# A linear-attention block and its MLP: rows of four steps, the two lowest levels inside a row

## The chip, the cores and the metric

The kernel runs on one core of a Trainium2 chip. The metric is device time in microseconds of one execution; lower is better. All times of the kernel before come from three runs and from one profiled execution.

## What is computed

Inputs r, k, v, w have the shape (batch 4, heads 8, steps 768, head size 48), u is (8, 48). The result of the attention, its heads side by side, is x of shape (4, 768, 384), and a normalized MLP of width 1536 is added to it.

```python
for t in range(S):
    cur = einsum('bhd,bhe->bhde', u[None] * k_t, v_t)
    y[:, :, t] = einsum('bhd,bhde->bhe', r_t, state + cur)
    state = w_t[..., None] * state + einsum('bhd,bhe->bhde', k_t, v_t)
...
x = y.transpose(0, 2, 1, 3).reshape(B, S, H * D)
mu, var = x.mean(-1), ((x - mu) ** 2).mean(-1)
xn = (x - mu) / sqrt(var + 1e-06) * g_ln
out = x + maximum(xn @ w_ch1, 0) @ w_ch2
```

So a value of step s reaches the output of a later step t through the product of k_s, of r_t and of every w between them, and reaches its own step through u.

## The kernel before

**Blocks and rounds.** The steps of a batch are cut in two halves of 384 steps (`RN`, three tiles of 128). A half with all eight heads is a round; there are eight rounds, and a round has two units of four heads, each with two pairs of heads. Round 0 is worked in two parts, its first tile and the other two. Where the prediction speaks of blocks, it means rounds.

**Inside a tile.** A tile of 128 steps is two chunks of 64 (`C`). Within a chunk the matrix of weights between steps is built in six levels (`NLEV`). At level `lev` steps stand in groups of n = 2^lev, and the matrix gets the squares between each even group and the odd group after it. `quads` makes the products of k and r for all squares of a level in small-tile form on TensorE (48 products for a whole round), into one of two PSUM places named `a`. `keep` copies the wanted squares from PSUM into the matrix `A` in SBUF: level 0 by an AND with a mask, levels 1 to 4 with a predicated copy, and level 5 by `keep_last` on ScalarE. `grow` then multiplies half of k and half of r by the products of w over the neighbouring group, so that the next level can be made from them. These products of w, for groups of 1, 2, 4 up to 32 steps, are made by `totals` on VectorE or GpSimd; those over 64 steps are `decay`.

**Loading and turning.** `load` brings w, k and r in their natural order, steps on partitions, into the `nat` places; in rounds 0 and 1 each partition gets three neighbouring steps of a head, later one step of each tile. `turn` transposes all three on TensorE into `w`, `k`, `r` with two heads and their 48 numbers on partitions; ScalarE copies the result from PSUM. In rounds 0 and 1 a transpose takes two instructions.

**The own step.** `own` makes the products r k u of each step and adds them over the 48 numbers (three VectorE or GpSimd instructions for half a round). In rounds 0 and 1 `own_by_tile` writes the sums to DRAM and reads them back by tile. `own_term` multiplies them with v, and the outputs' last step adds this to what TensorE made (`x<-a,vo` in the profile).

**State and outputs.** `turn_k` turns k back, `states` makes the sums of k and v per chunk and `decay` carries them on; `outputs` takes the matrix `A` with v, and r with the states, into an `a` place. Then come normalization, three transposes a tile, and the MLP. From round 1 on the MLP's first matrix is used in three parts, one of which, `d`, is streamed from DRAM for each of its twelve pieces (`stream`), into the eight `rest` places. From round 5 on the second matrix is in three parts too. At the start the two matrices, 64-bit numbers in DRAM, are made into 32-bit numbers on ScalarE and VectorE (`convert`).

**Order.** Nothing is issued where it is written. Each step is an `Op` of the class `Plan`, with an engine or a choice of engines, a cost, what it reads and writes, the places it takes and a priority, 40 for each round plus a stage. `Plan.order` simulates the engines and picks the op with the lowest priority number among those that can start first. The order found this way is fixed for each engine, the DMA issues on SyncE (`SP`) among them. The table `SHIFTS` moves priorities, by their whole number. Products with two operands in SBUF on VectorE and GpSimd are kept apart in time (`port`). In the first 90 us, where TensorE would wait, it runs filler products named `idle`. All instructions go through `InOrder`, so the profile shows line 50 for nearly all of them, and groups are told apart by tile names.

Of the kernel before, what the change touches and what calls it, by code (L numbers as in the profile page):

```python
# [66 lines left out]
class Plan:  # L67
# [23 lines left out]
        -472: 60.5, -360: -211.5, -38: -20.5, -32: -113.5, -31: -113.5, -29: -113.5, -22: -111.5,  # L91
        -20: -12, -10: 118.5, -6: 46.5, 8: -1.5, 9: 93.5, 11: -340.5, 12: -313.5, 16: 6.5, 20: 17,
        22: -346.5, 38: 25.5, 43: 250.5, 44: -325, 47: 80.5, 48: -87, 50: 79.5, 52: 93, 54: 95,
        56: 134, 58: 6, 60: 40, 62: 32, 66: -60.5, 83: 279, 87: 298.5, 88: 39, 90: 33, 92: 89,
        98: -296.5, 100: 100.5, 128: 801.5, 134: -18.5, 141: 36, 142: 138.5, 168: -69, 169: -48.5,
        170: 4.5, 178: 16, 180: -201.5, 182: 54, 184: 37, 200: 340.5, 204: -34.5, 207: 134,
        208: 49.5, 212: 32, 214: 74.5, 215: 49, 216: 74, 218: 132, 222: 53.5, 224: 93.5, 230: -123,
        240: -9.5, 248: 43.5, 249: 42.5, 252: 22.5, 255: -165, 257: 67.5, 260: -19, 264: 82.5,
        279: -663, 280: -16, 287: 110.5, 288: -117.5, 289: -54, 290: -54, 300: -39, 319: -22,
        320: 23, 360: 32, 405: 3.5, 406: -23.5, 412: -3, 416: -338.5, 420: -11.5, 423: 397.5,  # L100
        450: -24.5, 453: 12, 455: -105, 458: -7.5, 459: -51, 461: 77, 479: 87.5, 490: -33, 494: -2,
        495: 21.5, 497: 100, 498: 34, 499: 46, 503: -129, 505: -47.5,
# [13 lines left out]
    def add(self, eng, cost, fn, r=(), w=(), new=(), pri=0, lat=0.0, size=0, port=None, tiled=False, count=0):  # L116
        costs = {eng: cost} if isinstance(eng, str) else dict(zip(eng, cost))
        pri += self.SHIFTS.get(math.floor(pri), 0.0) if pri > -600 else 0.0
# [24 lines left out]
    def order(self, busy, idle=None, until=0.0):  # L143
# [20 lines left out]
        def start_of(op, e):  # L164
            t = max(free[e], op.ready)
            tags = [tag for tag, _ in op.new]
            for tag in set(tags):
                n = tags.count(tag)
                if len(self.homes[tag]) < n:
                    return None  # L170
                if tag not in self.dynamic and self.queue[tag][0] != op.i:
                    return None
                t = max(t, sorted(self.homes[tag])[n - 1][0])
            if op.port:
                t = max(t, held["POOL" if e == "DVE" else "DVE"])
                if e == "POOL" and t < op.ready + self.PATIENCE:

                    if portless["DVE"] - t < 0.6 * op.costs[e]:
                        t = max(t, free["DVE"] + 0.3)
            return t  # L180
# [101 lines left out]
def kernel(  # L282
# [49 lines left out]
        "nat": 5, "w": 1, "k": 2, "r": 2, "tot": 1, "decay": 3, "rk": 1, "own": 2, "own_row": 1,  # L332
        "v": 2, "vx": 2, "vo": 2, "s": 2, "last": 3, "rx": 2, "sx": 2, "x": 3, "xn": 3,
# [6 lines left out]
    def tile_(tag, name, shape, dtype=F32):  # L340
# [5 lines left out]
        if tag == "nat" and name.startswith("nat_"):  # L346
            tiles[name] = nat_homes[plan.place[name]]
            return tiles[name]
# [16 lines left out]
    ROWS, ROW = 2, TT * D  # L365
    nat_homes = [homes.tile([P, NK * 2 * HP], F32, tag=f"nat{i}", name=f"nat{i}") for i in range(HOMES["nat"])]
    plan.hold("vo", "nat_r_0")
    tile_("vo", "nat_r_0", [P, NH * ROW])
    for name in ("nat_r_1", "nat_k_1", "nat_w_1", "nat_k_0", "nat_w_0"):
        plan.hold("nat", name)  # L370
        tile_("nat", name, None)
# [4 lines left out]
    u_bc = const.tile([P, H, D], F32, name="u_bc")  # L376
# [7 lines left out]
    own_d = [scratch.tile([RN, H], F32, name=f"own_d{i}") for i in range(ROWS)]  # L384
    w1_d = scratch.tile([FC, P, KC, P], F32, name="w1d")
    masks = [const.tile([P, C // 2], I8, name=f"mask{lev}") for lev in range(NLEV - 1)]
    first_mask = const.tile([P, C // 2], I32, name="mask_and")
    plan.hold("sx", "wide")
    wide = tile_("sx", "wide", [P, NP, TT, D]).rearrange("p r c d -> p (r c d)").bitcast(I8)
    wide = [wide[:, ts(lev, C)] for lev in range(NLEV - 1)]  # L390
# [8 lines left out]
    for nm in "wkr":  # L399
        POOL.memset(tiles[f"nat_{nm}_0"][:, 0 : HP - D], 0.0)  # L400
    for nm in "wk":
        POOL.memset(tiles[f"nat_{nm}_0"][:, NH * ROW :], 0.0)
    for t in [a_bufs[0]] + a_homes:
# [3 lines left out]
    def build_mask(lev):  # L407
# [8 lines left out]
        for i in range(2):  # L416
            rows = ds(C * i, C)
            half = wide[lev][rows, ds(C // 2 * i, C // 2)]
            if lev:
                POOL.tensor_copy(out=masks[lev][rows], in_=half)  # L420
            else:
                POOL.tensor_scalar_mul(first_mask[rows], half, -1.0)
# [17 lines left out]
    NA = U * NP  # L440

# [15 lines left out]
    def keys_of(nm, part, us=both_units):  # L457
        rnd, c0, _ = part
        return [(f"{nm}{rnd}", NP * uu + pr, c0) for uu in us for pr in pairs]
# [6 lines left out]
    GAP = HP - D  # L466

    def natural(nm, part, a):

        rnd, c0, _ = part  # L470
        if rnd == 0:
            return f"nat_{nm}_{c0}", a
        return f"nat_{nm}{U * rnd + a // NP}", a % NP

    def row_of(part):

        return part[2] * D, (GAP if part[2] == 1 else 0)

    def load_first(nm, part, eng, pri):
        _, c0, nc = part  # L480
        b, f = rounds[0]
        name = natural(nm, part, 0)[0]
        queue = SP if eng == "SP" else ACT
        row, margin = row_of(part)

        def go():
            queue.dma_start(
                out=tiles[name][:, margin : margin + H * row].rearrange("p (h x) -> p h x", h=H),
                in_=SRC[nm][b, :, ds(f * RN + c0 * P, nc * P)]
                .rearrange("h (p c) d -> p h (c d)", p=P),  # L490
            )

        plan.add(eng, 0.5, go, w=[name], r=[], pri=pri, lat=2.0 if c0 else 3.5, size=1.05 + 0.5 * (nc > 1))

    def load(nm, q):
        b, f, g = units[q]
        name = f"nat_{nm}{q}"

        def go():
            to = tile_("nat", name, None)  # L500
            if q // U < ROWS:
                SP.dma_start(
                    out=to[:, 0 : NH * ROW].rearrange("p (h x) -> p h x", h=NH),
                    in_=SRC[nm][b, ts(g, NH), ds(f * RN, RN)]
                    .rearrange("h (p c) d -> p h (c d)", p=P),
                )
                return
            for c in range(TT):
                SP.dma_start(
                    out=by_tile(to)[:, c, :, 0:D],  # L510
                    in_=SRC[nm][b, ts(g, NH), ds(f * RN + c * P, P)].rearrange("h p d -> p h d"),
                )

        cost_, size = (0.5, 1.05) if q // U < ROWS else (1.95, 1.6)
        plan.add(
            "SP", cost_, go, w=[name], new=[("nat", name)], pri=at(q // U, "wrk".index(nm)), lat=2.0 if q // U < ROWS else 2.5,
            size=size,
        )

    def by_tile(t):  # L520
        return t.rearrange("p (c h d) -> p c h d", c=TT, h=NH)

    def turn(nm, part, a0, na, stage):
        rnd, c0, nc = part
        name, ps = f"{nm}{rnd}", f"{nm}_ps{rnd}_{c0}_{a0}"
        rows = rnd < ROWS
        row, margin = row_of(part)

        def go():
            t = tile_("b", ps, [P, na * nc * P])  # L530
            for a in range(na):
                key, pr = natural(nm, part, a0 + a)
                for c in range(nc):
                    to = ts(a * nc + c, P)
                    if not rows:
                        both = by_tile(tiles[key])[:, c, ts(pr, 2)].rearrange("p j d -> p (j d)")
                        PE.transpose(t[0:PD, to], both[:, 0:PD], ident)
                        continue


                    at_ = 2 * pr * row + c * D + margin
                    second, first = ds(at_ + row - HP, PD), ds(at_, HP)
                    PE.transpose(t[0:PD, to], tiles[key][:, second], ident)
                    PE.transpose(t[0:HP, to], tiles[key][:, first], ident)

        def keep(e="ACT"):
            to = of(part, tile_(nm, name, [P, U, W])[0:PD].rearrange("p u t -> p (u t)"), P)
            to, ps_ = to[:, a0 : a0 + na], tiles[ps][0:PD].rearrange("p (a x) -> p a x", a=na)
            if rows and nc > 1:
                to = to.rearrange("p a (s c) -> p a s c", c=nc)  # L550
                ps_ = ps_.rearrange("p a (c s) -> p a s c", c=nc)
            (DVE.tensor_copy if e == "DVE" else ACT.copy)(out=to, in_=ps_)

        n = na * nc
        keys = [(name, a0 + a, c0) for a in range(na)]
        new = [(nm, name)] if a0 == c0 == 0 else []
        plan.add(
            "PE", 0.11 * n * (1 + rows), go, count=2 * n * (1 + rows),
# [1134 lines left out]
```

## Time and profile before

| | |
|---|---|
| median of three runs | 523.19 us (520.78 to 523.92) |
| profiled execution, span from first to last instruction | 521.5 us |
| granted TensorE clock | 1.00 |
| DMA: packets, bytes moved | 122361, 55.84 MB |
| packets under 512 bytes | 93984 |
| HBM read, written | 45.05 MB, 7.10 MB |

The time of the profiled execution is not listed apart from its span; the median lies 1.7 us above the span. The page's first part gives the busy time of each engine and its share of the span; the second cuts the span into 40 slices of 13 us, one digit each, in tenths. In a group of instructions, out and in are named by tile, then partitions x elements, the count, busy time, mean ns of one, and the idle time of the engine before them with what ended it. Durations of neighbouring instructions on one engine overlap somewhat, so the distance between starts is the better price of one among many.

### The profile page before, as it was taken

What the parts mean: (1) busy time and instruction counts of PE and PEld (TensorE: products, weight loads), DVE (VectorE), ACT (ScalarE), POOL (GpSimd) and SP (SyncE); (2) the same over time, 40 slices, a digit from 0 to 9 for tenths busy, and PEclk for the clock granted to TensorE, in tenths of its full rate; (3) what the DMA queues carried; (4) which work ended last, traced back from release to release, by engine and by line L of the source; (5) the groups of instructions that cost most, each with busy time, mean ns of one, the idle gap of its engine ahead of it and who ended that gap; (6) DMA issues with size and microseconds to landing.
All of it is one profiled execution on the core that took longest, in us unless ns stands there. A gap on an engine that the chain in (4) does not pass through costs nothing.

```text
span 521.5 us, 20493 instructions
## 1 busy us (share of the span) xinstructions
PE 510.5 (98%) x8994; PEld 431.8 (83%) x8994; DVE 370.5 (71%) x786; ACT 270.4 (52%) x603; POOL 48.9 (9%) x80
## 2 busy tenths in 40 slices
PE   9999999998999999999999999999999999999995
PEld 6878987676987778987669886699767999999995
DVE  5899999889777799497858863397783655545334
ACT  3788888884463273584117543385841434333231
POOL 7212120133000001000100100000000000000000
PEclk9999999999999999999999999999999999999999
DMA  9886884287902385373625332023012312223101
GB/s 221 230 204 161 195 223 143 62 185 190 230 3 49 67 214 129 85 146 84 123 59 122 68 92 77 22 88 61 15 63 75 93 56 87 85 62 121 47 0 47
DMA packets 122361, 55.84 MB, mean 107 GB/s; under 512 B 93984, under 2 KB 119200, under 8 KB 122272
## 3 DMA queue, kind: packets, MB, share of 16 engines
q1 hardware_dynamic: 119152, 53.54, 40.7%
q10 hardware_dynamic: 3120, 0.98, 1.0%
q8 instruction: 71, 1.16, 0.9%
q14 instruction: 18, 0.15, 0.1%
HBM read 45.05 MB, written 7.10 MB: 100 GB/s over the span
## 4 chain that ended last, share of the span: by engine, by line
PE 92%; DVE 5%; DMA 1%; issue 1%; ACT 0%; SPq 0%; DVEq 0%; ACTq 0%
PE h_ps L50 30%; PE a L50 25%; PE o L50 22%; PE w_ps L50 3%; PE k_ps L50 2%; PE idle L50 2%; PE o_2P L50 2%; PE r_ps L50 2%; PE kn_ps L50 2%; PE xT_ps L50 1%; PE o_2D L50 1%; DVE x L50 1%; DVE r L50 1%; DMA d<-w1d 1%; DVE k L50 1%
## 5 line engine op out<-in xcount | busy, mean ns | idle before, releaser
L50 PE MATMUL o<-ffn,h 128*128 128x384 f32 x360 | 124.5, 490 | 1.0 <-PE h_ps L50 1.0
L50 PEld LDWEIGHTS o<-ffn,h 128*128 128x128 f32 x360 | 65.4, 190 | 38.7 <-PE h_ps L50 1.3
L50 PEld LDWEIGHTS a<-r,k 48*48 48x48 f32 (+5 forms) x4608 | 63.2, 126 | 14.1 <-issue 6.9
L50 ACT ACTIVATE h_ps<-h_ps 128x384 f32<-128x384 f32 x84 | 39.9, 475 | 65.8 <-PE h_ps L50 62.9
L50 PE MATMUL a<-r,k 48*48 48x32 f32 (+5 forms) x4608 | 69.4, 212 | 0.9 <-issue 0.8
L50 PE MATMUL h_ps<-xhl,wl 128*128 128x384 f32 x252 | 59.8, 345 | 0.0
L50 DVE SCALAR_TENSOR_TENSOR hL<-h_ps,hH 128x384 fp32r<-128x384 f32 x36 | 20.0, 556 | 53.9 <-ACT hH L50 53.7
L50 PE MATMUL h_ps<-xhl,wh 128*128 128x384 f32 x252 | 57.5, 335 | 0.0
L50 PE MATMUL h_ps<-xd,d 128*128 128x384 f32 x252 | 54.7, 345 | 2.1 <-DMA d<-w1d 1.8
L50 DVE TENSOR_TENSOR k<-k,tot 112x768 f32<-112x768 f32 (+1 forms) x50 | 40.0, 802 | 19.1 <-PE a L50 18.9
L50 PEld LDWEIGHTS h_ps<-xd,d 128*128 128x128 f32 x252 | 43.5, 188 | 4.0 <-issue 1.8
L50 PEld LDWEIGHTS h_ps<-xhl,wl 128*128 128x128 f32 x252 | 44.2, 188 | 1.6 <-ACT h_ps L50 0.4
L50 PEld LDWEIGHTS h_ps<-xhl,wh 128*128 128x128 f32 x252 | 45.0, 188 | 0.0
L50 ACT ACTIVATE h<-h_ps 128x384 f32<-128x384 f32 (+2 forms) x72 | 31.4, 437 | 26.2 <-PE h_ps L50 25.4
L50 DVE COPY_PREDICATED A<-mask,a 128x768 f32<-128x768 int8 (+2 forms) x36 | 39.3, 1095 | 3.6 <-PE a L50 2.8
L50 ACT ACTIVATE hH<-h_ps 128x384 fp32r<-128x384 f32 x36 | 17.7, 491 | 45.9 <-PE h_ps L50 45.7
L50 DVE TENSOR_TENSOR r<-r,tot 112x768 f32<-112x768 f32 (+1 forms) x50 | 39.9, 799 | 0.0
L50 ACT COPY r<-r_ps 112x384 f32<-112x384 f32 (+1 forms) x31 | 14.2, 493 | 24.5 <-PE r_ps L50 24.0
L50 PE MATMUL h_ps<-xf,w 128*128 128x128 f32 (+1 forms) x144 | 25.9, 331 | 0.0
L50 PE MATMUL a<-w2d,hD 128*128 128x384 f32 x72 | 24.4, 342 | 0.0
L50 PEld LDWEIGHTS a<-v,A 64*64 64x64 f32 x384 | 20.6, 133 | 4.4 <-issue 2.1
L50 PE MATMUL a<-w2h,hH 128*128 128x384 f32 x72 | 24.2, 337 | 0.0
(115 smaller groups left out, 953.4 us busy)
## 6 DMA issues: line engine op xcount, KB each, us to landing
d<-w1d SPq DMA_DIRECT2D x84, 192.0 KB, 2.9
raw<-in_moe_w_ch_dram SPq DMA_DIRECT2D x24, 384.0 KB, 4.3
v<-in_v_dram SPq DMA_DIRECT2D x48, 96.0 KB, 3.2
out_dram<-x SPq DMA_DIRECT2D x24, 192.0 KB, 1.9
nat<-in_w_dram SPq DMA_DIRECT2D x36, 96.0 KB, 3.5
nat<-in_k_dram SPq DMA_DIRECT2D x36, 96.0 KB, 3.2
nat<-in_r_dram SPq DMA_DIRECT2D x36, 96.0 KB, 3.5
w1d<-w1diff SPq DMA_DIRECT2D x12, 192.0 KB, 2.8
```

Source lines behind the costliest of these rows:

```text
L50: ins = self.tc.keep_in_program_order(f(*args, **kw))
```

## The change

**Rows of four.** w, k and r are loaded with four neighbouring steps of a head on a partition (`Q = 4`, 768 bytes in one piece), heads and groups of steps on the 128 partitions: 32 groups of four steps for each of four heads, in `nat_w`, `nat_k`, `nat_r`, one place each. A DMA brings one tile of four of the eight heads.

**Inside a row.** The new function `inner` makes on VectorE or GpSimd, on the natural layout, all that the levels 0 and 1 made: k and r multiplied by the w's inside their group of four (`pad_k`, `pad_r`), the product of four w (`w4`), and the sums over the 48 numbers for the step itself (with u), for its neighbour, and for the pairs two apart. These values (`vals`) go to DRAM and back in all rounds (`inner_by_tile`) and `place` sets them into `A` with a mask, as 4 x 4 squares on the diagonal.

**What falls away.** `quads`, `grow` and `keep` begin at level 2 (`LOW = 2`); `totals` too. `own`, `own_by_tile` and `own_term` go; the outputs are copied from PSUM to x by ScalarE or VectorE with no sum. Of w only `w4` is transposed (`turn_w`, three transposes a round), and k and r take 12 each in every round.

**Order.** `SHIFTS` has new values and is looked up by the op's number.

```diff
-        pri += self.SHIFTS.get(math.floor(pri), 0.0) if pri > -600 else 0.0
+        pri += self.SHIFTS.get(len(self.ops), 0.0)
...
-            if op.port:
+            if op.port and e in held:
...
+    def load(nm, part, queue="SP"):
...
+            for j in range(2):
+                engine.dma_start(
+                    out=tile_("n" + nm, name, None)[:, c, j].rearrange("p s d -> p (s d)"),
+                    in_=SRC[nm][b, :, ds(f * RN + c * P, P)][j::2].rearrange("a (k s) d -> a k (s d)", s=Q),
+                )
...
+        mult(
+            apart_one, lambda: k_()[:, 0::2], lambda: r_()[:, 1::2], half, 0.0,
+            r=raw["k"] + raw["r"], w=[rk], new=[("rk", rk)],
+        )
+        mult(
+            lambda: padded("k", part)[:, 0::2], lambda: k_()[:, 0::2], lambda: w_()[:, 1::2],
+            half, 0.1, r=raw["k"] + raw["w"], w=pad["k"][:1], new=[] if c0 else [("pk", f"pad_k{rnd}")],
+        )
...
+        mult(k_, k_, r_, 2 * half, 0.25, r=raw["r"], w=raw["k"])
+        mult(
+            k_, k_, lambda: u_bc[:, cs].rearrange("p c (s j) d -> p s (c j) d", s=1), 2 * half, 5,
+            r=[("u_bc", c) for c in range(c0, c0 + nc)], w=raw["k"],
+        )
...
+        def out_(j):
+            SP.dma_start(
+                out=d[j, c0 : c0 + nc].rearrange("c p x -> p c x"),
+                in_=tiles[name][:, tiles_no(part), j, 0 : Q * Q],
+            )
+
+        def back(j, rows, to):
+            src = d[j].rearrange("c (a k) (s t) -> (k s) (c a) t", a=NA, t=Q)[rows]
+            SP.dma_start(
+                out=tile_("va", va, [P, 2, TT * NA, Q])[to, j, NA * c0 : NA * (c0 + nc)],
+                in_=src[:, NA * c0 : NA * (c0 + nc)],
+            )
...
+            DVE.tensor_tensor(out=to, in0=v_, in1=m, op=ALU.bitwise_and)
...
+            for s in range(Q):
+                PE.transpose(
+                    t[0:PD, ts(s, P)], tiles[pad][:, s, c].rearrange("p j d -> p (j d)")[:, 0:PD], ident
+                )
...
-        for lev in range(NLEV):
+        for lev in range(LOW, NLEV):
```

## The prediction

> **What bounds the kernel now.** I read the page's totals and slices first, then the chain of waits, then three stages of the span, then single instructions.
>
> From the page: span, busy time by engine, the slices of PE, DVE and ACT, and the chain that ended last.
>
> ```profile
> span 521.5 us, 20493 instructions
> PE 510.5 (98%) x8994; PEld 431.8 (83%) x8994; DVE 370.5 (71%) x786; ACT 270.4 (52%) x603; POOL 48.9 (9%) x80
> ...
> PE   9999999998999999999999999999999999999995
> ...
> DVE  5899999889777799497858863397783655545334
> ACT  3788888884463273584117543385841434333231
> ...
> PE 92%; DVE 5%; DMA 1%; issue 1%; ACT 0%; SPq 0%; DVEq 0%; ACTq 0%
> ```
>
> PE is busy throughout and carries 92% of the chain, so PE work that goes away should shorten the span, unless the PE was not what set the pace at that place. DVE, and less so ACT, are nearly full too in the first ten slices (to about 130 us). So I asked for three stages; 126.7 us is where the chain has its last wait for a load of `d` before the second block's MLP starts, and 405 us is the end of the last attention output. Columns: stage, length, busy time (and instructions) of PE, weight loads, DVE, ACT, POOL, clock, DMA share, GB/s.
>
> ```profile
> 0.00:126.70 126.70, 124.66 (x2604) 99.48 (x2604) 111.51 (x259) 97.19 (x225) 32.52 (x63) 1.00 0.73 179
> 126.70:405.00 278.30, 274.70 (x5756) 222.57 (x5755) 202.19 (x419) 135.32 (x299) 15.35 (x17) 1.00 0.38 91
> 405.00:521.50 116.50, 111.13 (x637) 109.78 (x636) 56.83 (x111) 37.93 (x79) 1.02 (x1) 1.00 0.22 67
> ```
>
> Middle: PE is idle 3.6 of 278.3 us, DVE 76 us. Front: PE is idle 2.0 us, but 13.8 of its busy time are the `idle` filler products (34 of them, all before 50 us), so 16 us were spare, while DVE worked 111.5 of 126.7. The front is held by DVE and by chains through it, the middle by PE alone. The end is MLP only and untouched by the change.
>
> The Trainium skill (Perfetto Trace Analysis, Identifying the Most-Contended Engine) calls matmul busy time a poor measure and prefers weight-load busy time; that is 83% here, and read so, the PE would have slack and the middle would give nothing (the forecast would be about 516). The starts of the instructions below decide for me: they follow each other without a gap.
>
> PE in order of time inside the middle stage: start, length, operation, count.
>
> ```profile
> 186.08 1.15 PE L50 MATMUL xT_ps<-ident,xn 128*128 128x128 f32 x9
> 187.16 1.58 PE L50 MATMUL a<-r,k 48*63 48x32 f32 x96
> 188.67 0.79 PE L50 MATMUL kn_ps<-ident,k 112*128 112x112 f32 x6
> ...
> 191.92 1.56 PE L50 MATMUL a<-r,k 48*62 48x32 f32 x96
> 193.41 0.54 PE L50 MATMUL w_ps<-ident,nat 128*112 128x128 f32 x3
> 193.79 2.10 PE L50 MATMUL o<-ffn,h 128*128 128x384 f32 x6
> 195.73 1.15 PE L50 MATMUL w_ps<-ident,nat 128*112 128x128 f32 x9
> 196.71 2.10 PE L50 MATMUL o<-ffn,h 128*128 128x384 f32 x6
> 198.74 1.52 PE L50 MATMUL a<-r,k 48*60 48x32 f32 x96
> ```
>
> Start to start, the two lowest levels (48*63 and 48*62) take 1.51 and 1.49 us, and nine transposes 0.98 us, 0.109 each. Six `o` products take 1.94 us, but 2.03 before a level: entering the small-tile form costs 0.09.
>
> **What the change takes from PE.** Levels 0 and 1: 1.51 + 1.49 + 2 x 0.09 = 3.18 us per block, eight blocks. Transposes: blocks 2 to 7 have 36 each (12 of w, k, r), blocks 0 and 1 have 72 (their rows need a pair for each); 2 x 72 + 6 x 36 = 360, which are the 120 each of `w_ps`, `k_ps` and `r_ps`. After, a block has 12 of k, 12 of r and 3 of w, 27. So blocks 2 to 7 save 9 x 0.109 = 0.98 and blocks 0 and 1 save 45 x 0.109 = 4.9. Sum: blocks 2 to 7, 6 x (3.18 + 0.98) = 25.0 us, where PE alone holds the pace: taken in full. Blocks 0 and 1, 2 x (3.18 + 4.9) = 16.2 us, in the front: bounds 0 and 16.2.
>
> **What it does to DVE.** Durations, whole blocks:
>
> ```profile
> L50 DVE TENSOR_TENSOR k<-k,tot 112x768 f32<-112x768 f32 x35 | 33.4, 953 | 17.3 <-PE a L50 17.2
> L50 DVE TENSOR_TENSOR rk<-rk,u_bc 128x576 f32<-128x576 f32 x13 | 9.8, 755 | 2.2 <-POOL rk L50 2.0
> L50 DVE TENSOR_TENSOR x<-a,vo 128x288 f32<-128x288 f32 x28 | 11.4, 450 | 11.8 <-PE a L50 11.7
> ```
>
> Removed per block: four `grow` of two levels, 4 x 0.953 = 3.81; `keep` of levels 0 and 1, 0.953 + 1.88 (the level-1 one at 85.42 us) = 2.83; two totals 0.953 + 0.557 = 1.51; `own`, two halves of three steps, 6 x 0.755 = 4.53; `own_term` 2 x 0.755 = 1.51; four sums into x, 1.80, which become copies that ACT may do. Together 16.0. Added: eight products of 576 elements, 6.04; one of 288, 0.45; two of 1152, by the slope between 576 and 768 (0.198 for 192) 0.755 + 3 x 0.198 = 1.35 each, 2.70; sums over 1152, 1152 and 576, 3.45; two `place` of 768, 1.91. Together 14.55. Net -1.45 per block, -11.6 in all; -2.9 in blocks 0 and 1. POOL may take some products in both versions (rk there took 1.42); were all of POOL's 33 us of such work to fall to DVE at about half its price, +17, DVE would be at 376 of some 490 us, 77%, still not the bound of the middle.
>
> **ACT.** Per block away: four evictions of w and eight of k and r, 12 x 0.483 = 5.8. Added: six evictions of 512, 0.585 each, 3.5; one of w4, 0.48; two copies of 576 (0.483 and 0.585 at 384 and 512 give 0.64), 1.3, unless POOL has them; four copies of x, about 0.43 each, 1.7. Net +1.2, at 49% busy in the middle: nothing. In the front ACT is 77% busy: bound 0 to 2.4.
>
> **Loads.** For blocks 2 to 7 a DMA of w, k or r is 96 KB in pieces of 48 numbers, 192 bytes, 512 pieces; it becomes 128 pieces of 768 bytes. Hidden either way except at the start: first loads landed after 3.6 to 8.5 us. 0 to -2, taken 0, for before the first transpose now stand about ten DVE products of 192 elements (the 256-element ones start 0.34 apart), 3 us, where there were none.
>
> **New waits.** The diagonal values go to DRAM and back in every block (two writes, three reads; before, one pair in blocks 0 and 1 only). Write and read on SP, and what the pair took:
>
> ```profile
> own_d<-own_row SPq DMA_DIRECT2D x1, 12.0 KB, 3.0
> own<-own_d SPq DMA_DIRECT2D x1, 12.0 KB, 2.9
> ```
>
> The reads come in 16-byte pieces, 3072 per block. The mean packet took 28.5 ns (40.7% of 16 engines x 521.5 us over 119152 packets), so 3072 on 16 engines are 5.5 us: a trip is 5.9 to 11.4 us. The Trainium skill (DMA: Bandwidth & Descriptors, Specifications) puts full rate at 512 bytes or more and warns of read-modify-write below; it speaks for the new loads and against these pieces, and gives no price. On SP the reads wait for the writes, and behind them stand the loads of `d`, for which PE now waits 1.8 us in all: 0 to +6 over the run, taken 0, as eight `rest` places run ahead. On DVE `place` waits for the reads; behind it, in order, stand all `keep` and `grow`. I take 0 in the middle: transposes of w for block 2 ran at 104 us and its outputs at 172, so a block's front has some 68 us to hide 11 in.
>
> **The front.** DVE has 2.9 us less, and its waits before `k<-k,w` (level 0, 4.2 us in the first 125) go with level 0. I take 7.1 of the possible 16.2; the rest becomes filler. The new order by instruction number moves everything and no row prices it: from -3.6 (PE's idle time in the middle) to +8, taken 0.
>
> Sum: 25.0 + 7.1 = 32.1 off a span of 521.5 gives 489.4. The runs' median is 1.7 above that span, so **491 us**. Bounds of this case: 16.2 instead of 7.1 and the order's 3.6 give 478; 0 in the front and +8 give 506.
>
> **Rivals.** (1) The front follows PE fully: 523.2 - 41.2 = 482. For: fewer levels in the opening chain. Against: DVE at 88% there. 15%. (2) The front gives nothing and DVE queues stall the middle now and then (past 130 us DVE still has slices at 9 tenths: the 15th, 16th, 18th and 27th of the 40): half of the 25 gained, 505 to 515. 9%. (3) Slower: the trip through DRAM is exposed in each block. There are two `a` places in PSUM; levels 2 and 3 fill both until `place` lets `keep` empty them, and then no small-tile product can start. Price: up to 11.4 us x 8 = 91 against 32, 582; it decides from 4.0 us exposed per block, and at 6 gives 539. For: DMA was 73% busy in the front. Against: the 68 us of lead. 8%. (4) The order eats what is saved, 518 to 528: 5%. My forecast, 484 to 505, has the remaining 63%.
>
> **Numbers.** A measurement here can tell about 1%. Faster by more (below 518): 63 + 15 + 9 = 87%; same 5%; slower 8%. The range 478 to 508 leaves out (3), (4) and half of (2).
>
> **What would show it.** Right: no `a<-r,k` products of 48*63 or 48*62, 3072 `a<-r,k` in place of 4608, 24 `w_ps` transposes; PE busy near 470 with filler of about 20 us or more; the middle, up to the last attention output, shorter by about 25. Wrong: PE waits with `place` or a DMA as releaser; DVE above 85% past 130 us; filler beyond 35 us.

## The result, and the profile after

The changed kernel takes 596.4 us (595.0 to 597.4, four runs). The kernel before took 523.3 us (520.8 to 523.9) beside it. The ratio is 1.143, with a 95% interval of 1.138 to 1.147: 73 us slower, where 32 us faster was forecast. The profiled execution has a span of 594.4 us.

From the page of the changed kernel, the same lines as those shown of before: span, busy time by engine, slices of TensorE and of the granted clock, and the shares of the chain that ended last.

```profile
span 594.4 us, 17275 instructions
...
PE 520.7 (88%) x7374; PEld 426.4 (72%) x7374; DVE 370.9 (62%) x766; ACT 270.6 (46%) x596; POOL 64.0 (11%) x81
...
PE   7597699669987987998599796899999899999997
...
PEclk9789789969988898999698898799999999999999
...
PE 52%; DMA 18%; SPq 13%; DVE 12%; ACT 2%; issue 2%; DVEq 0%; ACTq 0%
```

Two things are to be seen. TensorE has 1,620 instructions fewer than before (the trace has two for each of the 48 small products of a level and round, so 96) and is busy longer, 520.7 us against 510.5: 39.6 us of it are filler (13.8 before), and the clock, which was granted in full throughout before, dips in many slices (0.93 in the mean). And the chain, 92% TensorE before, now runs for 31% through transfers and through `SPq`, SyncE's own line of DMA issues.

The longest waits of TensorE and VectorE in the changed kernel (engine and tile, what it waited for: us in total, times, longest):

```profile
DVE A L50 <- DMA va<-own_d: 26.3, 10, 5.6
PE a L50 <- DVE A L50: 22.0, 6, 9.6
PE w_ps L50 <- DVE w L50: 18.8, 3, 8.2
DVE pad_k L50 <- DMA own_d<-vals: 10.9, 1, 10.9
DVE rk L50 <- DMA nat_k<-in_k_dram: 9.9, 2, 6.8
```

TensorE waits for VectorE, and VectorE for two kinds of transfer: the loads of w, k and r, and the own values on their way through DRAM. `va<-own_d` before `A` is the wait of `place`, and TensorE's 22.0 us for `A` stand behind it: the sign that the prediction named for being wrong.

The start, from the timeline of the changed kernel (start, length, instruction; in brackets the idle time before it and what ended it):

```profile
4.59 6.06 ACTq L50 DMA_DIRECT2D nat_w<-in_w_dram  x4
...
10.21 0.36 DVE L50 TENSOR_TENSOR rk<-nat_k,nat_r 128x192 f32<-128x192 f32 x1 [6.76 <-DMA nat_k<-in_k_dram]
...
17.75 0.35 ACT L50 COPY pad_k<-nat_k 128x192 f32<-128x192 f32 x1 [15.45 <-DMA nat_w<-in_w_dram]
...
20.86 0.46 PE L50 MATMUL k_ps<-ident,pad_k 128*112 128x128 f32 x1 [4.12 <-DVE pad_k L50]
```

The first product on VectorE starts at 10.2 us, for k has not landed; ScalarE makes its first copy at 17.8 us, behind its own issues of loads, four of which took 6.06 us; k is turned at 20.9 us, where before it was turned at 8.1. The transfers' share tells why. From the transfers' view of the first 26 us, in 40 slices (tenths of the 16 DMA engines busy, and GB/s):

```profile
DMA  0001122222222222223828222222222224424424
GB/s 0 0 0 26 40 82 86 93 85 83 87 86 85 83 83 84 82 76 80 190 94 196 87 84 83 85 85 85 89 85 85 80 87 112 113 85 111 111 85 96
```

For most of it the digit is 2 and some 85 GB/s come in. The digit stands for 20 to 30% of sixteen engines, 3.2 to 4.8 of them, so these loads seem to keep no more than four busy. Experiment 1 tests this.

### The profile page after: what moved, and what is told of

Read it like the earlier page. It is cut to its first block, busy times and chain, and to the rows that moved or that the text cites. A ratio compares the mean times of both kernels' runs of the same rounds, so it can differ in the third digit from the quotient of the medians.

```text
span 594.4 us, 17275 instructions
## 1 busy us (share of the span) xinstructions
PE 520.7 (88%) x7374; PEld 426.4 (72%) x7374; DVE 370.9 (62%) x766; ACT 270.6 (46%) x596; POOL 64.0 (11%) x81
## 4 chain that ended last, share of the span: by engine, by line
PE 52%; DMA 18%; SPq 13%; DVE 12%; ACT 2%; issue 2%; DVEq 0%; ACTq 0%
PE h_ps L50 19%; PE a L50 14%; SPq L50 13%; PE o L50 13%; DMA raw<-in_moe_w_ch_dram 4%; DMA nat_k<-in_k_dram 4%; DMA nat_w<-in_w_dram 2%; PE o_2P L50 2%; DMA own_d<-vals 2%; DVE vals L50 2%; DMA nat_r<-in_r_dram 2%; DMA d<-w1d 2%; DVE k L50 2%; DMA u_bc<-in_u_dram 1%; DVE r L50 1%
## 5 line engine op out<-in xcount | busy, mean ns | idle before, releaser
L50 PE MATMUL o<-ffn,h 128*128 128x384 f32 x360 | 134.7, 517 | 0.0
L50 PEld LDWEIGHTS o<-ffn,h 128*128 128x128 f32 x360 | 68.6, 200 | 38.1 <-issue 5.8
L50 PEld LDWEIGHTS a<-r,k 48*60 48x60 f32 (+3 forms) x3072 | 42.3, 128 | 33.7 <-DVE A L50 17.3
L50 PE MATMUL a<-r,k 48*60 48x32 f32 (+3 forms) x3072 | 46.4, 213 | 22.1 <-DVE A L50 15.2
L50 PE MATMUL h_ps<-xhl,wh 128*128 128x384 f32 x216 | 51.4, 348 | 0.0
L50 PE MATMUL idle<-nought 128*128 128x384 f32 (+2 forms) x94 | 39.6, 570 | 1.0 <-DVE eps L50 1.0
L50 PE MATMUL a<-v,A 64*64 64x48 f32 x384 | 26.6, 234 | 9.6 <-DVE A L50 6.2
L50 DVE TENSOR_TENSOR r<-r,tot 112x768 f32<-112x768 f32 (+1 forms) x40 | 33.9, 850 | 0.0
L50 DVE TENSOR_TENSOR A<-va,mask_and 128x768 int32<-128x768 int32 (+2 forms) x18 | 16.1, 892 | 26.5 <-DMA va<-own_d 26.3
L50 DVE TENSOR_TENSOR pad_k<-nat_k,nat_w 128x576 f32<-128x576 f32 (+2 forms) x8 | 5.7, 717 | 40.7 <-DMA own_d<-vals 10.9
L50 PEld LDWEIGHTS idle<-nought 128*128 128x128 f32 x94 | 20.9, 237 | 14.1 <-issue 7.4
```

The lines of the kernel that those rows point to most:

```text
L50: ins = self.tc.keep_in_program_order(f(*args, **kw))
```

## The experiments

All were made on the changed kernel. Times are medians; with one run it is said.

**1. Loads over more engines.** A load takes four heads times 32 rows, and its outermost loop was the heads. Here the partitions are numbered row group first, head second, so that the outermost loop is 32; the evictions and the load of u follow. The writes of the own values had to be cut by tile, six per block instead of two.

```diff
-  ...[j::2].rearrange("a (k s) d -> a k (s d)", s=Q)
+  ...[j::2].rearrange("a (k s) d -> k a (s d)", s=Q)
-  ap=[[2 * D, NA], [0, NB], [1, 2 * D]]
+  ap=[[0, NB], [2 * D, NA], [1, 2 * D]]
```

> The changed kernel (596 us), with the partitions of the row loads numbered group-of-steps first, head second, so that the outermost dimension of a load of w, k or r has 32 entries and not 4; u likewise; the write of the own values split by tile to keep its place in DRAM. Same bytes, same order of all other work. Theory A (the row loads move at some 85 GB/s because their outermost dimension is the 4 heads and only 4 of the 16 DMA engines work): 480 to 510 us, granted clock near 1.00, DVE's waits for nat_k, nat_w and nat_r nearly gone. Theory B (the trip of the own values through DRAM is exposed): 580 to 600 us. Theory C (the new order by itself makes PE wait): 580 to 600 us.

557.5 us (553.9 to 561.3), ratio 1.070 (1.064 to 1.077): 39 us less, by the order of the loops alone (that of the load of u, at the start, among them) and with more DMAs. But it is not the 480 to 510 us that theory A gave: the loops of the loads are one part of the loss, and another part is left. The same view of its first 26 us:

```profile
DMA  0003969769499897797425697156999979999537
GB/s 0 0 0 82 273 177 254 203 156 70 54 287 270 174 328 234 176 300 204 95 38 66 80 364 136 14 52 123 369 402 272 200 301 278 349 322 249 104 42 100
```

Over the 26 us the engines are 74% busy and move 180 GB/s (84 in the changed kernel). The first product of VectorE starts at 5.2 us, not 10.2.

**2 and 3. No trip of the own values,** on the changed kernel (2) and with the loads spread (3): the writes to DRAM, the reads and their waits go, and `place` sets zeros.

```diff
-  def out_(j): SP.dma_start(...)
+  def out_(j): pass
...
-  v_ = tiles[va].bitcast(I32)
+  v_ = va_still.bitcast(I32)
```

> The changed kernel without the trip of the own values through DRAM: no writes, no reads, and the diagonal 4 x 4 squares of the weight matrix are left zero (so the own step and the steps within a row of four are missing from the result). Loads unchanged. Theory A (4 DMA engines for the row loads): 560 to 596 us. Theory B (trip exposed): 480 to 520 us, since PE's 22 us of waits for A and what follows from them go. Theory C (order): 580 to 596 us.

> Both edits: loads over all engines and no trip (the diagonal 4 x 4 squares are left zero). Against the spread loads alone this prices the trip once the loads are quick. Theory A: within 5 us of the spread loads alone. Theory B: some 20 us or more below it.

571.0 us and 517.3 us (one run each). So the trip costs 25 us with the loads as in the change and 40 with the spread ones; spreading is worth 39 with it and 54 without it. The two costs aren't independent, and without either the kernel is at about the time of before, not at 491. Taking out the trip also takes its DMAs out of SyncE's line, five per block in experiment 2 and nine in 3, so its price includes what other loads wait behind them.

How such a wait arises is seen on SyncE in the kernel of experiment 1, in the second block's front (start, length of all issues in a row, what, how many), and on VectorE at the same place:

```profile
75.61 2.49 SPq L50 DMA_DIRECT2D nat_w<-in_w_dram  x4
...
79.49 4.67 SPq L50 DMA_DIRECT2D own_d<-vals  x6
84.21 1.25 SPq L50 DMA_DIRECT2D nat_r<-in_r_dram  x2
85.50 3.74 SPq L50 DMA_DIRECT2D nat_k<-in_k_dram  x4
89.28 0.59 SPq L50 DMA_DIRECT2D va<-own_d  x1
89.92 2.70 SPq L50 DMA_DIRECT2D nat_r<-in_r_dram  x4
92.66 1.31 SPq L50 DMA_DIRECT2D va<-own_d  x2
```

```profile
77.34 1.34 DVE L50 TENSOR_REDUCE vals<-nat_r 128x24 f32<-128x1152 f32 x1
...
91.65 0.76 DVE L50 TENSOR_TENSOR pad_k<-nat_k,nat_w 128x576 f32<-128x576 f32 x1 [6.64 <-DMA va<-own_d]
92.33 0.95 DVE L50 TENSOR_TENSOR A<-va,mask_and 128x768 int32<-128x768 int32 x1
```

SyncE issues without a pause, one DMA per 0.59 to 0.94 us (the means of these rows). The last own value is made at 78.68; its six writes are out by 84.16, but before the first read stand six loads of the following block, and four more before the other two reads. VectorE places the values at 92.33 and 96.08, and until 91.65 it had waited 6.6 us. From value to the first place it takes 13.7 us. The profile puts the wait down to the read. But the instruction that waited, `pad_k`, works on the loads of k and w, and the last load of k was issued at 88.6; such loads took 2.5 to 3.5 us to land in this stretch. So the read and the loads of the next block are late together, in one line.

**4. More work for TensorE.** The small products of level 2 are made twice, with the spread loads.

```diff
+  for _ in range(2 if lev == LOW else 1):
       PE.matmul(...)
```

> Spread loads, and the products of level 2 made twice into the same place (48 more small products, about 1.35 us, in each of 8 rounds, 11 us in all; same result). If PE sets the pace from the second round on, as my prediction had it: 8 to 12 us above the spread loads alone. If DVE or DMA sets it: 0 to 4 us above.

574.2 us (one run), 16.7 more than experiment 1, where 8 to 12 were expected if TensorE set the pace. TensorE's work at this place still counts in full, and somewhat over, although its waits are longer than before. So the saved products were not lost because TensorE had stopped to matter; other time was added to it.

**5. Fewer DMAs.** One load takes all eight heads of a tile, one write both halves of a tile's own values: 15 DMAs per block where experiment 1 had 27.

```diff
-  for j in range(2):
-      engine.dma_start(out=...[:, c, j]..., in_=SRC[nm]...[j::2].rearrange("a (k s) d -> k a (s d)", s=Q))
+  engine.dma_start(out=...[:, c]..., in_=SRC[nm]....rearrange("h (k s) d -> k h (s d)", s=Q))
```

> The first experiment's kernel (partitions numbered group first, head second), with the same bytes in fewer DMAs: one load brings a tile of all eight heads instead of four (9 loads per block instead of 18), and one write takes both halves of a tile's own values (3 writes instead of 6; 3 reads as before). 27 DMAs of w, k, r and own values per block become 15. Theory A (SyncE's issue queue: it hands out one DMA per 0.55 to 0.60 us, and the reads of the own values stand in line behind the next block's loads): 12 x 0.57 = 6.8 us of issue per block go, and the 557.5 us fall by 15 to 35, to 522 to 542; SPq in the chain falls from 18% to under 8%. Theory B (the trip's own two landings, 2.4 to 3.1 us each, hold VectorE in every block): these stay, so 550 to 558. Theory C (the order of instructions, found for other durations, is what is lost): 550 to 558 too.

536.6 us (536.0 to 539.2), ratio 1.030 (1.023 to 1.038): 21 us less than experiment 1, `SPq` 2% of the chain (18% there). This is theory A's range, but one dependency that I gave the reads (both writes) also changed the planner's order.

**6. The next block's loads behind the trip.**

```diff
+  r=[(f"va{rnd - 1}", i, ...) for i in range(3)] if rnd else [],
```

> The kernel with 15 DMAs per block, and the loads of w, k and r of a block may be issued only after the reads of the own values of the block before. Theory A: what is left of the queueing goes, 5 to 15 us below the kernel with 15 DMAs alone; no nat load stands between the writes and the reads of the own values. Theory B: same within 1%, for the two landings stay. A loss would say that the loads now come too late: VectorE then waits for nat_w, nat_k or nat_r at the start of a block.

575.9 us (574.2 to 577.0), 39 more than experiment 5: the loss that was left open there, and far larger than any figure. The loads cannot wait: those of a late block are issued from 343.8 us, after the reads of the own values at 336.4, and in the eight slices that follow (345 to 460 us) TensorE is busy for 2 to 7 tenths. The edit also gives the planner another order, so the 39 us aren't all the loads'.

**7. The table `SHIFTS` empty,** on experiment 5.

```diff
-  pri += self.SHIFTS.get(len(self.ops), 0.0)
+  pri += 0.0
```

> The kernel with 15 DMAs per block with the table SHIFTS taken as empty, so that the order is what the planner's priorities alone give. Theory C (the table was found for other durations and now harms): faster than the kernel with 15 DMAs by 5 us or more. Theories A and B: the table is still worth something, 0 to 25 us slower.

549.5 us (one run), 13 more. Theory C falls: the table still helps.

**8. No trip, on experiment 5.** The edit is that of experiment 2.

> The kernel with 15 DMAs per block, without the trip of the own values: they are neither written nor read back, and the 4 x 4 squares on the diagonal of the matrix of weights are left at zero. It leaves out that part of the result. The same without the fewer loads took 517.3 us. If the loads' issues cost nothing once the trip is gone, 515 to 519; if they hold the front back, 505 to 514. Its distance to the kernel with 15 DMAs is what the trip still costs there: theory A 5 to 25 us, theory B 35 to 40.

533.3 us (one run), 3.3 less than with the trip. With 15 DMAs per block, in this order, the trip costs almost nothing. But the kernel is 16 us above experiment 3, which has no trip either and more DMAs. The difference left is the order of instructions; experiment 9 tests that.

**9. Experiment 5 with the order of the change.** All three writes go out at the first of their two places, so that the planner sees what it saw in the changed kernel; TensorE, VectorE and ScalarE run the same instructions in the same order as there. The dependency of the reads, against experiment 5:

```diff
-  r=[(*key, 0), (*key, 1)]
+  r=[(*key, j)]
```

> The kernel with 15 DMAs per block again, but with the instruction order of PE, DVE and ACT kept as it is in the changed kernel (all three writes of own values are issued at the first of their two places, so the planner sees what it saw before; in the earlier kernel with 15 DMAs a changed dependency gave another order). Theory A (SyncE's queue of issues was what exposed the trip): close to the 517.3 us of spread loads without the trip, 515 to 523; the 16 us between the two kernels without the trip (517.3 and 533.3) were the order. Theory B (the trip's landings, or the fewer and larger loads themselves, hold the kernel): 530 to 540, as the earlier kernel with 15 DMAs.

517.5 us (514.8 to 520.8), ratio 0.991 (0.987 to 0.994). This is 40 us less than experiment 1, and experiment 3's 517.3 with the trip in place. Its page, and SyncE's line and VectorE at the same place:

```profile
span 515.4 us, 17183 instructions
...
PE 64%; DVE 17%; DMA 11%; SPq 5%; issue 2%; ACT 0%; POOL 0%; DVEq 0%; ACTq 0%; POOLq 0%
```

```profile
75.03 1.96 SPq L50 DMA_DIRECT2D own_d<-vals  x3
77.03 0.63 SPq L50 DMA_DIRECT2D nat_r<-in_r_dram  x1
77.71 1.96 SPq L50 DMA_DIRECT2D nat_k<-in_k_dram  x2
79.83 0.48 SPq L50 DMA_DIRECT2D va<-own_d  x1
80.36 1.50 SPq L50 DMA_DIRECT2D nat_r<-in_r_dram  x2
81.90 1.33 SPq L50 DMA_DIRECT2D va<-own_d  x2
```

```profile
73.66 1.34 DVE L50 TENSOR_REDUCE vals<-nat_r 128x24 f32<-128x1152 f32 x1
...
82.38 0.76 DVE L50 TENSOR_TENSOR pad_k<-nat_k,nat_w 128x576 f32<-128x576 f32 x1 [0.95 <-DMA nat_k<-in_k_dram]
83.13 0.96 DVE L50 TENSOR_TENSOR A<-va,mask_and 128x768 int32<-128x768 int32 x1
```

The values are ready at 75.00 and the first are placed at 83.13: 8.1 us instead of 13.7, with the same neighbours in the line, but half as many writes and loads. VectorE's wait before it is 0.95 us, for a load of k, and not 6.6. TensorE's wait for `A` fell from 22.0 us in the changed kernel to 3.3.

So the form of its DMAs costs the change 79 us (596.4 against 517.5), more than its whole loss of 73; the rest of it, the trip through DRAM included, is worth a gain of about 1%. What the trip still costs in this order was not run.

**10. No loads from ScalarE.** The first block's loads that ScalarE issued go to SyncE.

```diff
-  engine = SP if queue == "SP" else ACT
+  engine = SP
```

> As the kernel before it in this call, but the first block's loads that ScalarE issued (k of the first part; w and r of the second) are issued by SyncE. Without the trip, ScalarE's first copy stood behind its ten issues until 10.3 us, and VectorE waited 3.3 us for it. If that holds the front back, ScalarE's first copy starts before 8.5 us and the time falls by 1 to 5 us against the other kernel; if the loads' landings hold it (SyncE now has all of them in line), 0 to 4 us slower.

515.9 us (513.9 to 520.0), ratio 0.990 (0.986 to 0.993). ScalarE's first copy starts at 4.7 us, as expected, but the 1.6 us lie inside the spread of the runs: not told apart from none.

**11 and 12. What holds the front.** In experiment 10 TensorE has 33 us of filler, and with its waits 38.1 us without real work before 50 us, where the kernel before had 15.5. Experiment 11 cuts the filler; experiment 12 also leaves out the own values of the first block.

```diff
-  out.append((free["PE"], lambda n=n, home=home: idle[2](n, home[1])))
+  n_ = 20 if free["PE"] == busy["PE"] else -(-n // 2)
+  out.append((free["PE"], lambda n=n_, home=home: idle[2](n, home[1])))
```

```diff
   def go(e):
+      if rnd == 0 and at_ in (0.0, 0.25, 0.3, 5): return
```

> The kernel with 15 DMAs per block and all loads on SyncE (515.9 us), with the filler products of TensorE cut: the first run of them from 28 to 20 units of 128 columns, every later one to half. There the transpose of w for the first part ran at 9.69 us, though VectorE had made its input by 6.87, for the filler ended only then. Theory D (the front is late in part because the filler, sized for another load time, stands in the way): the transpose starts near 7 us and the time falls by 2 to 4 us. Theory E (VectorE's longer chain in the first block holds the front, the filler only fills the gap): 0 to 1 us less. If the clock falls in the gaps: up to 6 us slower, with a granted clock below 1 before 50 us.

> The kernel with the shorter filler, without the own values of the first block: its products for them, their sums and their trip are left out, and the 4 x 4 squares of that block stay zero (this part of the result is missing). By single instructions this takes 9.5 us from VectorE in the first 35 us. Theory E: if VectorE holds the front, 5 to 9 us faster than the kernel with the shorter filler. Theory D alone: 0 to 2 us.

518.9 us (516.6 to 524.2) and 517.1 us (514.9 to 518.9). In experiment 11 the transpose of w did start at 7.6 instead of 9.7, and nothing came of it: the transposes of the second part's k stand at 23.94 (23.75 in experiment 10). With 8.4 us less VectorE work they stand at 22.31, and that too is lost again by 45 us (the level-4 products start at 44.8 and 45.2). From the stages of the three kernels, 26 to 50 us (experiments 10, 11 and 12; columns as in the prediction):

```profile
26.00:50.00 24.00, 20.95 (x461) 14.34 (x460) 21.12 (x57) 19.70 (x48) 2.21 (x3) 1.00 0.81 245
26.00:50.00 24.00, 17.52 (x423) 12.21 (x426) 20.56 (x54) 18.49 (x46) 2.39 (x4) 0.86 0.81 242
26.00:50.00 24.00, 19.39 (x434) 12.77 (x433) 18.34 (x51) 18.16 (x45) 0.00 (x0) 0.79 0.70 221
```

In experiment 12 VectorE has more time to spare and ScalarE is as busy as in 11. But with the shorter filler the granted clock is 0.86 and 0.79 here, 1.00 in experiment 10: the drop that the expectation named as a possible loss. So neither theory got its gain, but a gain from VectorE's shorter chain may have been lost to the clock; these two runs don't rule out theory E.

**13 and 14. SyncE's first issues.** In experiment 12 the chain ran for the first 14 us along SyncE's issues, 0.61 us each, and then through a load of the MLP's matrix. Experiment 13 lets ScalarE issue seven of them, experiment 14 lets GpSimd issue all 24 loads of the matrices (`POOL` in place of the choice in the diff).

```diff
-  SP.dma_start(out=u_bc...)
+  ACT.dma_start(out=u_bc...)
-  SP.dma_start(out=tile_("raw", ...
+  (ACT if i < 4 else SP).dma_start(out=tile_("raw", ...
```

> The kernel with 15 DMAs per block and all loads on SyncE (515.9 us), with seven of the first issues taken off SyncE: the three of u and the first four of the MLP's matrix are issued by ScalarE. Theory F (the front is late because SyncE hands out its first 20 DMAs at 0.61 us each, 14 us, before the matrix for the MLP starts to come): seven issues are 4.3 us, the second part's k lands 2 us earlier, and the time falls by 2 to 5 us. Theory E (VectorE's chain holds the front): 0 to 1 us. A loss of 1 to 3 us if ScalarE's copies now stand behind its issues.

> As the kernel before it in this call, but all 24 loads of the MLP's two matrices are issued by GpSimd, and the three of u by ScalarE. Theory F: 27 x 0.6 = 16 us of issue leave SyncE's line in the first 130 us; the time falls by 3 to 7 us against 515.9. Theory E: 0 to 1 us. If an issue on GpSimd, which must also make products there, takes longer than on SyncE, its products and the VectorE work behind them come later, up to 5 us slower.

515.3 us (511.4 to 519.3), ratio 0.988 (0.985 to 0.992), and 516.2 us (512.0 to 522.5), ratio 0.989 (0.987 to 0.992). Neither is told apart from experiment 10. Theory F falls as a single cause too: in experiment 13 the chain runs through the filler and the trip of the own values (3.8 us for the write, 4.5 for the read) instead. In experiment 10, where the filler is whole, the chain runs the same way to the second part's k (start, length, what):

```profile
14.03 2.73 DMA own_d<-vals
16.77 4.26 DMA va<-own_d
...
21.13 0.42 DVE A L50
...
23.75 1.07 PE k_ps L50 x8
```

So in the front the trip of the first part's own values is not hidden: the product that the second part's transposes of k need stands behind `place` on VectorE, which ran at 21.13 when the read had landed. Without that trip, in experiment 12, these transposes start 1.6 us earlier than in experiment 11.

The best of these kernels are about 1% faster than before and 14% faster than the change as made.

## Why the prediction was wrong

**The step that failed** is the one on the loads: "it becomes 128 pieces of 768 bytes. Hidden either way except at the start", priced at 0 to -2 us. I looked at the length of a piece and not at the order of the loops around it. With the heads outermost the transfers kept about a quarter of the sixteen engines busy, 85 GB/s. A block's rows are 18 x 96 KB = 1.77 MB, at 85 GB/s an estimate of 21 us on those four engines, 167 us in eight blocks. Experiment 1 shows what it cost: 39 us. The Trainium skill has the rule (DMA: Bandwidth & Descriptors, Why a DMA increments its semaphore by 16 and not by 1): the number of engines is the largest up to 16 that divides the slowest dimension of both sides, where that is not 1. It gives 4 for the change's loads and 16 for the spread ones. The busy shares, digit 2 against 74%, agree with that. I had read that page for the size of pieces alone.

**The step on the trip** failed in its second half. Its length was right: 5.9 to 11.4 us were given, and value to place took 8.1 where the line is short. But "I take 0 in the middle" rested on 68 us of lead that the own values don't have, and the wait was looked for on the wrong side. I priced what stands behind the reads on SyncE, the loads of `d`. What cost was SyncE's line ahead of them: the loads of the next block, at some 0.6 us each, stand before the reads, and are themselves behind the writes. With 15 DMAs per block in place of 27, in the same order of the other engines, 40 us go (experiments 1 and 9). Rival (3) had the sign and the place, `place` on VectorE, and gave it 8%; the lower of its two prices, 6 us a block, is near what experiment 1 shows against 3, 40 us or 5 a block. It had the wrong mechanism, the trip itself and not the line, and nothing of the loads, so its upper price of 582, near the measured 596, is near by luck. Before, as many loads went through the line in blocks 2 to 7 (18 each), but no read of own values stood behind them.

**The order** was taken at 0 between -3.6 and +8. Experiments 5 and 9 run the same DMAs in two orders of the other engines and differ by 19 us, so such bounds are too narrow. What the change's own order costs against the order of before no run shows.

**TensorE's saving** was nearly right. Without filler, its work is 496.7 us before (510.5 - 13.8) and 459.7 in experiment 10 (492.9 - 33.2): 37.0 less, of a possible 41.2 (25.0 and 16.2). Experiment 4 shows that work added at level 2 still counts.

**The front** is the other step that was mis-sized, and it is most of the 25 us between experiment 10 and the forecast. I let it take 7.1 of 16.2 us, so that time without real work would grow by 9.1. Up to 50 us it grew by 22.6 (38.1 against 15.5) and from there to 130 us by 3.6 (5.0 against 1.4). The step counted VectorE's total work there, not that k and r can be turned only after their products, and that those of the second part stand behind the trip of the first: the first `k_ps` starts at 12.0 us in experiment 10, the second part's at 23.75, where before they came at 8.1 and 14.0. What would shorten this stays open. The filler, VectorE's work with it, and SyncE's issues were relieved, and no such run was faster than experiment 10 by more than 0.6 us. Several paths may end nearly together, and the lower clock may have hidden a gain; no run relieved all of them at a full clock.

**VectorE** was to lose 11.6 us and lost none in the change (370.9 against 370.5) and 2.7 in experiment 9. Two terms were mis-sized: of the first products of k and r in `own`, two in each block, VectorE had only six whole ones and a smaller one before and GpSimd the rest (an estimate of some 7 us too much counted as removed, at 0.755 each), and half of the outputs' copies, which I gave to ScalarE, ran on VectorE (7.4 us; the 14 largest 6.2). Smaller terms that go the other way were not taken apart. It was not the bound of the middle, as said.

## What to carry to other kernels

Before pricing a DMA by its bytes and the length of its pieces, look at its outermost loop and at the busy share of the engines: here two tenths, with these loads waited for, were loads that left most of the engines idle. SyncE's line had a price of some 0.6 us per issue; count the DMAs per round, and what stands ahead of the one that is waited for. When a change to a tuned kernel loses, keep its order of instructions while the suspected parts are changed one at a time, else the order's own swing, here 16 to 19 us, hides the answer.

## What was not expected of the hardware

TensorE's granted clock, 1.00 in the mean before, was lower where TensorE waited: 0.64 in the mean of the changed kernel's stage from 13 to 26 us, where TensorE was busy for 8.9 us of 13, filler included, and 0.93 over the span. Without filler, the same products took 481.1 us there (520.7 - 39.6) and 459.7 in experiment 10 at 0.99: some 21 us more, a second price of the waits. How much of it reached the whole time no run separates. And an issue on SyncE takes about as long for 192 KB (0.63 us, one of `nat_r` in experiment 9) as for 96 KB (1.25 us for two in experiment 1), so half as many DMAs of twice the size take about half the line.
